# Keys turned in four full blocks, the last low block of v in full products, and the order planned anew

## The chip, the core and the metric

The program runs on one core of a Trainium2 chip. Its engines work side by side, each through its own queue in order: TensorE (PE, with its weight loads as PEld), VectorE (DVE), ScalarE (ACT), GpSimd (POOL), and SyncE (SP), which only issues transfers. The metric is device time of one execution in microseconds; less is better.

## The reference, cut to what matters

```python
def _attn_ref(q, k, v, g_q, g_k):            # 8 batches, 12 heads, 448 positions, head size 64
    q_n, k_n = rmsnorm(q, g_q), rmsnorm(k, g_k)
    scores = scale * np.matmul(q_n, k_n.transpose(0, 1, 3, 2))
    attn = np.exp(scores - np.max(scores, axis=-1, keepdims=True))
    attn = attn / (np.sum(attn, axis=-1, keepdims=True) + 1e-09)
    return np.matmul(attn, v)

def _moe_ref(x, w_in, conv_w, w_out):        # x: 8 x 448 x 768, w_in: 768 x 1024
    h = np.maximum(x @ w_in, 0.0)
    conv_out = ...                           # three taps along the sequence, one weight per column
    gate = 1.0 / (1.0 + np.exp(-conv_out))
    return h * gate @ w_out
```

The twelve heads of a batch are laid side by side to make its x.

## The kernel before

Two heads are worked on together; there are 48 such pairs, six to a batch. Most matrix products are done in float16 with operands that are split into a high and a low part, so that one product becomes three (high by high, low by high, high by low).

For pair n the steps are, by their names in the code:

- `load_k`, `load_q`, `square`, `square_sum`, `rsqrt` (nine small operations on 16 or 32 columns, numbered 0 to 8, each on DVE or POOL), `apply_rms`: the rows are normalised.
- `qk_transpose(n, 1)` turns the keys on TensorE, `qk_transpose(n, 0)` the queries, in four blocks each; 448 keys make three blocks of 128 rows and one of 64. `qk_hi` and `qk_lo` bring the result out of PSUM.
- `scores(n, g)` for g from 0 to 3: the products of queries and keys. Groups 0 to 2 use the two 64-row halves of the array at once, one head in each (the profile's form 64*128); group 3 uses the whole array.
- `soft_max` (DVE), `soft_exp` (ACT), and for pairs 10 to 47 `p_hi`, `p_lo` and `p_turn` (split the probabilities and turn them by a transfer). Pairs 0 to 9 are turned on TensorE by `p_transpose`, and `p_evac` brings them out.
- `pv(n, k)`: the product with v. Each matmul makes 64 columns of the result, one head in each 64-column half of the array, so they go in couples (form 128*64). For pairs 10 to 47 the table `PV7` lists eleven couples: block number, high or low part of v, and how many rows. Its entry for the low part of block 3 has 64 rows, the others 128.
- `sum_transpose` and its followers, `x_scale`, `x_hi`, `x_lo`: the sums and the pair's part of x.

For batch b, `in_part` is x by `w_in`, then `in_relu`, `in_conv`, `in_tanh`, `in_gate`, `in_hi`, `in_lo`, and `out_part` is the product with `w_out`.

All steps draw on eight PSUM banks. The order on every engine is not written out. A planner at the end of the function takes each step's due time (from the table `PH`), what it needs (`needs`), the engines it may run on and an estimate of its cost (`options`), and picks step by step. It adds 0.09 to a TensorE step whose `mode` differs from that of the step before. What it settles is fixed before the program runs: each engine then follows its list and waits where a list makes it wait. The engine that a step runs on comes from the same choice.

The last block of the keys' rows that is not filled by keys is set to zero once (`z[HALF[1], 1, :, :, 3]`), and `v_load` fills the matching rows of v's block 3 with the same 64 rows a second time.

Of the kernel before, what the change touches and what calls it, by code (L numbers as in the profile page):

```python
# [10 lines left out]
F32 = mybir.dt.float32  # L11
# [8 lines left out]
PH = dict(  # L20
    T0=10.967, N0=6, T=15.459, ti=17.476, si=5.11, so=8.471, hop=0.482, beta=0.03, wi0=-42.913,
    wi1=123.322, wo0=27.142, wo1=142.983, cw=-10.8, tg=-97.576, tl=35.262, ea=0.79, te=113.425,
    ep=0, hs=0, nf=3, adj=0.139, nz=8, ne=0, sc=5, tc=2, mc=8, p_qe=0.885, p_evac=1.078,
    p_hi=1.427, p_lo=9.771, p_rms=1.35, p_v=0.784, p_x=0.724, p_g=1.806, p_relu=0.483,
    p_cv=0.454, p_qz=0.683, p_ev=2.488, sp=0.083, nbulk=16, p_rs=0.002, p_sq=1.249, p_w=0.964,
    v0=-5.914, dg=7, n1=10, sw=-0.025, nl=4, tj=0.658, hk=0, pvs=1, pk=0.1, p_sa=0.456,
    p_ph=0.558, p_pl=0.0, nq=3, nk=94, p_qh=0.287, p_ql=0.313, tq=9.136, ti0=0.38, ti1=-0.226,
    ti2=-0.488, ti3=0.474, ti4=-0.143, ti5=0.702, ti6=0.881, ti7=-2.49, si0=1.104, si1=1.725,
    si2=1.798, si3=1.468, si4=1.613, si5=1.143, si6=1.624, si7=1.691, to0=0.944, to1=0.306,
    to2=-1.453, to3=-1.281, to4=-0.007, to5=-0.844, to6=-0.745, to7=-1.059, so0=1.501, so1=1.467,  # L30
    so2=1.988, so3=1.424, so4=1.513, so5=0.757, so6=0.754, so7=0.218, pg=0.05,
    dq=[-3.68, -0.12, 0.27, 2.41, 3.7, 2.72, 2.35, -4.24, 0.69, 8.02, -0.69, 3.34, -0.75,
# [3 lines left out]
    da=[-0.05, 0.22, 0.68, 2.21, 3.37, -3.05, -1.7, -0.58, -2.92, 0.62, 2.69, -0.09, 4.89,  # L36
# [3 lines left out]
    dv=[-1.03, -0.52, -1.1, -1.21, -4.04, -5.21, -6.35, 4.57, 7.65, 3.51, 2.52, -1.82,  # L40
# [3 lines left out]
)  # L44
# [22 lines left out]
def tile_attention_moe(ctx: ExitStack, tc, q, k, v, g_q, g_k, w_in, conv_w, w_out, out):  # L67
# [343 lines left out]
    def square_sum(n):  # L411
        m = duo(n)[0]
        w = D // 2 if halved(n) else D
        if m == n:
            new("st", n, [P, 4, duo(n)[1], 2, 2 * NB], F32)
        nc.vector.tensor_reduce(  # L416
            old("st", m)[:, 0, n - m].rearrange("p i s -> p (i s)"),
            old("sq", n).rearrange("p i h t d -> p (i h t) d")[..., :w], axis=AX.X, op=ALU.add,
        )
# [90 lines left out]
    def qk_transpose(n, i):  # L510
        ps = new_bank("t", ("qk", n, i))
        x = slots(n, i).rearrange("p t h d -> p t (h d)")
        for t in range(NB):
            m, w = (min(P, S - t * P), P) if i else (PB, PB)
            nc.tensor.transpose(ps[:, t * w : t * w + m], x[:m, t], ident[:m, :m])  # L515

# [148 lines left out]
    def nd(n):  # L665
        return 0 if n < PH["n1"] else PH["dg"]
# [125 lines left out]
    def sum_load(n, h):  # L792
# [10 lines left out]
    PV7 = (  # L803
        *((c, 0, P) for c in range(4)), *((c, 1, 64 if c == 3 else P) for c in range(4)),
        *((c, 0, P) for c in (4, 5, 6)),
# [333 lines left out]
    def needs(name, *a):  # L1139
# [300 lines left out]
    def options(name, *a):  # L1440
# [29 lines left out]
            apply_rms=lambda: [dve(0.68)] if a[0] < PH["ep"] else [pool(1.14), dve(0.68)],  # L1470
            qk_transpose=lambda: [pe(0.48)],
            apply_gain=lambda: [pool(1.14), dve(0.68)],
# [19 lines left out]
            sum_load=lambda: [dma("rb", 0.75)],  # L1492
            pv=lambda: [pe(2 * PV_STEP * 0.00082 * (S - nd(a[0]) * P // 2) if a[1] < NB else (0.77, 0.77, 0.58)[a[1] - NB])],
            x_scale=lambda: [dve(0.64)],
# [11 lines left out]
            in_carry=lambda: [dve(0.18), act(0.3)],  # L1506
            out_part=lambda: [pe(0.665)],
            out_evac=lambda: [act(0.58), dve(0.6)],
# [89 lines left out]
    free = dict.fromkeys(waiting, 0.0)  # L1598
    pmode = None

    def mode(name, *a):

        return name if name == "pv" or name == "scores" and a[1] != NG - 1 else ""

# [3 lines left out]
    def vacant(step, e, dma, t):  # L1608
# [64 lines left out]
    while len(order) < len(steps):  # L1673
        best = None
        for e, ws in waiting.items():
            pick = None
            for step, (t, _, dma) in ws.items():
                t = max(t, free[e])
                if dma and step[0] in BULK and len(bulk) >= PH["nbulk"]:
                    t = max(t, bulk[-PH["nbulk"]])  # L1680
                t, spots = vacant(step, e, dma, t)
                if t > 1e8:
                    continue
                sw = 0.0
                if e == "PE" and mode(*step) != pmode:
                    t += 0.09
                    sw = PH["sw"]
                elif locks(e, step[0], *step[1:2]):
                    t = max(t, port["DVE"] - PH["pk"] if e == "POOL" else port["POOL"] + PH["pg"])
                key = t + sw + (BETA if e != "SP" else PH["sp"]) * urgency(step), urgency(step), steps[step][1]  # L1690
                if pick is None or key < pick[0]:
                    pick = key, t, step, spots
            if pick and (best is None or pick[1] < best[0]):
                best = *pick[1:], e
# [88 lines left out]
```

## Time and profile before

| | |
|---|---|
| timed runs | 863.71, 863.99, 869.9 us; median 863.99 us |
| the profiled execution, from its first instruction to its last | 866.6 us |
| TensorE, matmuls in flight | 810.0 us, 5416 matmuls |
| DVE, ACT, POOL busy | 663.1, 680.0, 632.9 us |

The page gives each engine's busy time, the chain of work that ended last, and groups of instructions. Views of the trace give stretches of it: a row of a timeline has the start and the length of a run of instructions of one kind, so the difference between the starts of two rows that follow each other is what the first of them cost the engine. A matmul's own length in the trace is longer than that, since matmuls overlap in the array.

### The profile page before, as it was taken

The numbers are of one execution on the slowest core, as the hardware profiler recorded it, in microseconds if no ns is written. First come the engines' busy times: TensorE is split into PE (matmuls) and PEld (weight loads), VectorE is DVE, ScalarE is ACT, GpSimd is POOL, SyncE is SP. The second block draws the span as 40 slices with busy tenths as digits, with TensorE's granted clock in tenths as the row PEclk, the third lists the DMA queues.
The fourth block names the chain that finished last, engine by engine and source line by source line (L and its number), as shares of the span: only waits on it lengthen the run. The fifth ranks groups of instructions, "written<-read, shape, count | busy, mean of one in ns | idle before, by whom it ended". The sixth has DMA issues, their size and how long they took to land.

```text
span 866.6 us, 16129 instructions
## 1 busy us (share of the span) xinstructions
PE 810.0 (93%) x5416; PEld 416.0 (48%) x5416; DVE 663.1 (77%) x1100; ACT 680.0 (78%) x1476; POOL 632.9 (73%) x849
## 2 busy tenths in 40 slices
PE   0688899999999799999999999999999999999998
PEld 0244444544444355455445545545454555445554
DVE  5799889887888988888788887687888767772530
ACT  1689678987998888888899879889879788884541
POOL 6436647787889788887888788888889877974210
PEclk9999999999999899999999999999999999999999
DMA  8963844136989989996998899789998997566001
GB/s 233 268 203 73 204 120 81 36 79 128 196 181 186 189 159 194 172 185 142 214 185 143 171 203 200 149 171 171 195 194 142 175 171 143 115 106 131 37 1 73
DMA packets 338446, 132.63 MB, mean 153 GB/s; under 512 B 301908, under 2 KB 332988, under 8 KB 337596
## 3 DMA queue, kind: packets, MB, share of 16 engines
q1 hardware_dynamic: 338364, 131.60, 74.3%
q8 instruction: 43, 0.70, 0.3%
q14 instruction: 39, 0.32, 0.1%
HBM read 58.22 MB, written 11.18 MB: 80 GB/s over the span
## 4 chain that ended last, share of the span: by engine, by line
PE 82%; DVE 7%; ACT 3%; DMA 3%; SPq 3%; issue 2%; POOL 0%; DVEq 0%; ACTq 0%; POOLq 0%
PE banks L999 25%; PE banks L920 24%; PE banks L695 12%; PE banks L846 10%; PE banks L515 4%; PE banks L837 4%; PE banks L757 2%; DMA v<-in_v_dram 2%; ACT e L710 1%; SPq L380 1%; DVE vacc L616 1%; PE banks L777 1%; SPq L1096 1%; ACT PT L93 1%; DVE ph L105 1%
## 5 line engine op out<-in xcount | busy, mean ns | idle before, releaser
L105 POOL TENSOR_TENSOR ph<-e,ph 128x768 f16<-128x768 f32 (+3 forms) x296 | 270.5, 936 | 40.6 <-ACT ph L93 26.9
L920 PE MATMUL banks<-x,wi 128*128 128x448 f16 x1152 | 248.1, 353 | 0.3 <-ACT e L710 0.3
L999 PE MATMUL banks<-wo,gring 128*128 128x384 f16 (+1 forms) x1056 | 211.0, 329 | 4.7 <-ACT e L710 4.4
L920 PEld LDWEIGHTS <-wi 128*128 128x128 f16 x1152 | 108.8, 98 | 99.6 <-issue 12.9
L93 ACT CAST ph<-e 128x1024 f16<-128x1024 f32 (+1 forms) x147 | 137.7, 938 | 3.2 <-DMA PT<-ph 1.2
L999 PEld LDWEIGHTS <-gring 128*128 128x128 f16 (+1 forms) x1056 | 101.8, 100 | 73.8 <-issue 17.1
L695 PE MATMUL banks<-kT,qT 64*128 64x448 f16 x864 | 105.9, 358 | 5.5 <-DVE qT L553 4.2
L105 POOL TENSOR_TENSOR sq<-qk,st 128x512 f32<-128x512 f32 x96 | 103.2, 1090 | 5.8 <-DVE st L438 4.4
L846 PE MATMUL banks<-PT,vp 128*64 128x448 f16 (+1 forms) x836 | 97.6, 363 | 1.2 <-issue 0.9
L515 PE MATMUL banks<-ident,sq 128*128 128x128 f32 (+1 forms) x364 | 60.3, 278 | 20.9 <-POOL sq L105 18.4
L416 DVE TENSOR_REDUCE st<-sq 128x16 f32<-128x1024 f32 x48 | 58.1, 1210 | 13.8 <-ACT sq L399 13.7
L846 PEld LDWEIGHTS <-vp 128*64 128x64 f16 (+1 forms) x836 | 41.3, 109 | 52.8 <-issue 33.7
L515 PEld LDWEIGHTS banks<-ident,sq 128*128 128x128 f32 (+1 forms) x364 | 43.6, 144 | 45.5 <-POOL sq L105 21.8
L105 POOL TENSOR_TENSOR x<-rB,x 128x448 f16<-128x448 f32 x48 | 50.0, 1042 | 19.9 <-ACT x L93 19.3
L695 PEld LDWEIGHTS <-qT 64*128 64x128 f16 x864 | 34.4, 95 | 59.0 <-issue 31.8
L757 PE MATMUL banks<-ident,e 128*128 128x128 f32 x280 | 44.3, 291 | 9.8 <-ACT PT L93 2.9
L999 PE MATMUL banks<-wo,wi 128*128 128x384 f16 (+1 forms) x192 | 50.3, 327 | 0.0
L399 ACT ACTIVATE sq<-qk 128x1024 f32<-128x1024 f32 x41 | 43.1, 1052 | 7.9 <-DMA qk<-in_q_dram 5.0
L853 DVE TENSOR_TENSOR rB<-banks,rB 128x448 f32<-128x448 f32 x48 | 29.7, 619 | 25.2 <-PE banks L846 14.9
L93 ACT COPY PT<-banks 128x512 f32<-128x512 f32 x64 | 36.5, 582 | 13.1 <-PE banks L757 10.6
L757 PEld LDWEIGHTS banks<-ident,e 128*128 128x128 f32 x280 | 32.8, 146 | 27.9 <-ACT PT L93 8.3
L562 POOL COPY qz<-qT 64x128 f16<-64x128 f16 x96 | 30.3, 315 | 16.5 <-DVE qT L553 11.7
(1129 smaller groups left out, 1627.7 us busy)
## 6 DMA issues: line engine op xcount, KB each, us to landing
rB<-rd SPq DMA_DIRECT2D x96, 112.0 KB
qk<-in_q_dram SPq DMA_DIRECT2D x23, 448.0 KB
wo<-in_moe_w_in_dram SPq DMA_DIRECT2D x6, 1024.0 KB
v<-in_v_dram SPq DMA_DIRECT2D x24, 256.0 KB
gring<-in_moe_w_out_dram SPq DMA_DIRECT2D x8, 768.0 KB
qk<-in_k_dram SPq DMA_DIRECT2D x23, 256.0 KB
v<-in_v_dram SPq DMA_DIRECT2D x24, 192.0 KB
qk<-in_k_dram SPq DMA_DIRECT2D x23, 192.0 KB
```

What stands on the lines that cost most here:

```text
L93: (nc.scalar.copy if e == "ACT" else elementwise(e).tensor_copy)(dst, src)
L105: elementwise(e).tensor_tensor(dst, a, b, op=op)
L399: nc.scalar.activation(sq, qk(n), AF.Square)
L416: nc.vector.tensor_reduce(old("st", m)[:, 0, n - m].rearrange("p i s -> p (i s)"), old("sq", n).rearrange("p i h t d -> p (i h t) d")[..., ...
L515: nc.tensor.transpose(ps[:, t * w : t * w + m], x[:m, t], ident[:m, :m])
L562: e.tensor_copy(z[HALF[h], :, HALF[h]], old("qT", n)[HALF[h], :, t0 : t0 + 64])
L695: nc.tensor.matmul(ps[u][:, :S], lhs, kt[r, w], start=(i == 0), stop=(i == 2))
L757: nc.tensor.transpose(ps[:, kt * P : (kt + 1) * P], e[:, k0 : k0 + P], ident)
L837: nc.tensor.matmul(ps[HALF[h], :S], v[r, h, k], pt[r, k, h * S : (h + 1) * S], start=(k == 0), stop=(k == NB - 1),)
L846: nc.tensor.matmul(ps[HALF[h], :S], v[:m, w, h, c % 4], pt[:m, c, h * S : (h + 1) * S], start=(i == 0), stop=(i == len(PV7) - 1),)
L920: nc.tensor.matmul(ps[:, :S], wi[:, wl, c, fc * P : (fc + 1) * P], old("x", b * NP + c)[:, xl], start=(i == 0), stop=(i == 3 * NP - 1),)
L999: nc.tensor.matmul(ps[p0 : p0 + m, :NO2], g, wo[:, wl, fc, half * NO2 : (half + 1) * NO2], start=(i == 0), stop=(i == 3 * NFC - 1),)
```

## The change

`qk_transpose` turns the fourth block of the keys with all 128 rows, where it took 64. `PV7` takes 128 rows for the low part of block 3. The planner's charge for a change of tiling is made anew: a step now has a mode at its beginning and one at its end. `needs` and `ORDER` say that some steps, such as `square_sum` of two pairs, keep their order, and all numbers of `PH` and some costs in `options` are others, so that the lists of all engines are made anew.

```diff
 PH = dict(
-    T0=10.967, N0=6, T=15.459, ti=17.476, si=5.11, so=8.471, hop=0.482, beta=0.03, wi0=-42.913,
+    T0=11.0661, N0=6, T=15.4646, ti=17.4515, si=5.1142, so=8.4623, hop=0.4923, beta=0.0299,
...
     def square_sum(n):
         m = duo(n)[0]
         w = D // 2 if halved(n) else D
-        if m == n:
-            new("st", n, [P, 4, duo(n)[1], 2, 2 * NB], F32)
+        if ("st", m) not in rings.setdefault("st", Ring(BUFS["st"])).d:
+            new("st", m, [P, 4, duo(n)[1], 2, 2 * NB], F32)
...
         for t in range(NB):
-            m, w = (min(P, S - t * P), P) if i else (PB, PB)
-            nc.tensor.transpose(ps[:, t * w : t * w + m], x[:m, t], ident[:m, :m])
+            m = P if i else PB
+            nc.tensor.transpose(ps[:, t * m : (t + 1) * m], x[:m, t], ident[:m, :m])
...
     PV7 = (
-        *((c, 0, P) for c in range(4)), *((c, 1, 64 if c == 3 else P) for c in range(4)),
+        *((c, 0, P) for c in range(4)), *((c, 1, P) for c in range(4)),
         *((c, 0, P) for c in (4, 5, 6)),
     )
...
             yield "square_half", n
+            yield "square_sum", n - 1
...
         elif name == "qk_hi":
+            yield ("x_turn" if turned(n - 1, a[1]) else "qk_hi"), n - 1, a[1]
...
-            qk_transpose=lambda: [pe(0.48)],
+            qk_transpose=lambda: [pe(0.44 if a[1] else 0.39)],
...
-            out_part=lambda: [pe(0.665)],
+            out_part=lambda: [pe(0.652)],
...
-    pmode = None
-
-    def mode(name, *a):
-
-        return name if name == "pv" or name == "scores" and a[1] != NG - 1 else ""
+    pmode = "T"
+
+    def modes(name, *a):
+
+        if name == "scores" and a[1] != NG - 1:
+            return "SS"
+        if name == "pv":
+            return "VQ" if a[1] == NB - 1 else "VV"
+        if name == "out_part" and a[0] % 2 and not a[1]:
+            return "VV"
+        return "TT"
...
     ORDER = {
+        ("qk_hi", "qk_hi"), ("x_turn", "qk_hi"), ("square_sum", "square_sum"),
...
-                if e == "PE" and mode(*step) != pmode:
-                    t += 0.09
+                if e == "PE" and modes(*step)[0] != pmode:
+                    t += 0.094
```

Three places show what becomes of the lists. The names behind an arrow are what an instruction reads, those ahead of it what it writes; line numbers after the change are seven higher up to the middle of the file.

First TensorE in the middle of the program, where the keys of a pair are turned between products with `w_out` (`sq` holds the normalised rows, `gring` the gated hidden layer). Before:

```order
L777 MATMUL banks<-ident,rsum_4297 7x128
L515 MATMUL banks<-ident,sq_4081 128x128 x3
L515 MATMUL banks<-ident,sq_4081 128x64
L999 LDWEIGHTS gring
L999 MATMUL banks<-wo_82,gring 128x384
```

And after, at a like place:

```order
L1006 LDWEIGHTS gring
L1006 MATMUL banks<-wo_82,gring 128x384
L522 MATMUL banks<-ident,sq_4059 128x128 x4
L522 MATMUL banks<-ident,sq_4059 128x112 x4
L702 LDWEIGHTS qT_4259
```

The block of 64 columns is gone, and the keys are four alike; here the queries' four blocks of 112 follow at once.

Second DVE at the start of the program, from the sum of squares of pair 0 on (`st` holds the sums and what `rsqrt` makes of them, `wi` and `wo` the words of the first weight that `convert` works on). Before:

```order
L451 TENSOR_TENSOR st_133<-st_133 128x16
L453 TENSOR_TENSOR st_133<-st_133 128x16
L438 SCALAR_TENSOR_TENSOR st_133<-st_133 128x16
L243 TENSOR_SCALAR wi_81<-wo_82 128x1024
L247 SCALAR_TENSOR_TENSOR wi_81<-wo_82,wi_81 128x1024
L251 SCALAR_TENSOR_TENSOR wi_81<-wo_82,wi_81 128x1024
L243 TENSOR_SCALAR wi_81<-wo_82 128x1024
```

And after:

```order
L458 TENSOR_TENSOR st_133<-st_133 128x16
L460 TENSOR_TENSOR st_133<-st_133 128x16
L250 TENSOR_SCALAR wi_81<-wo_82 128x1024
L254 SCALAR_TENSOR_TENSOR wi_81<-wo_82,wi_81 128x1024
L258 SCALAR_TENSOR_TENSOR wi_81<-wo_82,wi_81 128x1024
L445 SCALAR_TENSOR_TENSOR st_133<-st_133 128x16
L250 TENSOR_SCALAR wi_81<-wo_82 128x1024
```

`rsqrt` 4 of pair 0 has gone from DVE to POOL, and `rsqrt` 8, the last, has come from POOL to DVE, behind the three instructions of the first block of the weight; POOL has 4 to 7 now where it had 5 to 8, six instructions in either case.

Third DVE in pair 40, from `soft_max` of group 1 to that of group 2 (`sst` is its result, `c_` the convolution, `o_` an output row, `ph` the split probabilities). Before:

```order
L701 TENSOR_REDUCE sst_(40_1_7663<-banks 128x1 x2
L958 SCALAR_TENSOR_TENSOR c_(5_5_7557<-c_(5_5_7557,banks 128x448
L948 SCALAR_TENSOR_TENSOR c_(5_6_7640<-banks,cwb_7054,c_(5_6_7640 128x447 x2
L416 TENSOR_REDUCE st_7702<-sq_7649 128x16
L99 TENSOR_SCALAR o_(4_2_7717<-banks,vsc_4327 128x384
L701 TENSOR_REDUCE sst_(40_2_7723<-banks 128x2
```

And after:

```order
L708 TENSOR_REDUCE sst_(40_1_7633<-banks 128x1 x2
L955 SCALAR_TENSOR_TENSOR c_(5_5_7618<-banks,cwb_7062,c_(5_5_7618 128x447 x2
L910 TENSOR_TENSOR vsc_5483<-vsc_5483,wsc 128x1
L918 COPY vsc_4407<-vsc_5483 64x1
L919 COPY vsc_4407<-vsc_4407 64x1
L569 COPY qz_78<-qT_7566 64x2x64
L945 TENSOR_SCALAR banks<-banks 128x448
L112 TENSOR_TENSOR ph_71<-e_74,ph_71 128x2x3x128
L112 TENSOR_TENSOR ph_71<-e_74,ph_71 128x2x64
L708 TENSOR_REDUCE sst_(40_2_7696<-banks 128x1 x2
```

Both instructions of a `p_lo` (the rows with `ph`) and a `q_middle` (`qz`) stand on DVE now, between two `soft_max`; before, they were on POOL.

## Rows read from the trace of the kernel before

**Rows 1.** The page: an engine's busy time, and the chain that ended last.

```profile
PE 810.0 (93%) x5416; PEld 416.0 (48%) x5416; DVE 663.1 (77%) x1100; ACT 680.0 (78%) x1476; POOL 632.9 (73%) x849
...
PE 82%; DVE 7%; ACT 3%; DMA 3%; SPq 3%; issue 2%; POOL 0%; DVEq 0%; ACTq 0%; POOLq 0%
```

**Rows 2.** Windows: length, busy PE, PEld, DVE, ACT, POOL, granted clock, DMA.

```profile
0.00:309.00 309.00, 256.69 (x1615) 129.80 (x1617) 264.35 (x440) 246.66 (x548) 219.16 (x297) 0.98 0.70 156
309.00:862.00 553.00, 552.71 (x3803) 286.11 (x3798) 398.71 (x662) 432.73 (x928) 413.71 (x553) 1.00 0.78 152
...
195.00:290.00 95.00, 92.97 (x611) 46.08 (x612) 79.55 (x133) 85.08 (x186) 81.19 (x108) 0.98 0.90 172
275.00:308.00 33.00, 26.88 (x176) 12.32 (x175) 29.51 (x54) 28.42 (x63) 28.41 (x34) 0.90 0.96 182
290.00:402.00 112.00, 106.41 (x743) 53.64 (x740) 95.67 (x162) 95.94 (x208) 95.29 (x128) 0.97 0.92 178
```

**Rows 3.** Timeline of TensorE at 439 us: start, length, line, tiles, form, count.

```profile
439.12 0.73 PE L920 MATMUL banks<-x,wi 128*128 128x448 f16 x3
439.79 0.74 PE L695 MATMUL banks<-kT,qT 64*128 64x448 f16 x6
440.46 0.74 PE L920 MATMUL banks<-x,wi 128*128 128x448 f16 x3
441.04 0.73 PE L695 MATMUL banks<-kT,qz 128*128 128x448 f16 x3
```

**Rows 4.** Timeline of TensorE: four blocks turned, and the row behind.

```profile
145.44 0.60 PE L757 MATMUL banks<-ident,e 128*128 128x128 f32 x4
145.88 1.87 PE L920 MATMUL banks<-x,wi 128*128 128x448 f16 x9
...
558.28 0.69 PE L515 MATMUL banks<-ident,sq 128*128 128x128 f32 x4
558.90 0.34 PE L999 MATMUL banks<-wo,wi 128*128 128x384 f16 x1
```

**Rows 5.** Timeline of TensorE: couples of `scores` and of `pv`.

```profile
414.42 1.31 PE L695 MATMUL banks<-kT,qT 64*128 64x448 f16 x12
415.66 2.12 PE L999 MATMUL banks<-wo,gring 128*128 128x384 f16 x12
...
492.79 0.76 PE L846 MATMUL banks<-PT,vp 128*64 128x448 f16 x6
493.38 0.33 PE L999 MATMUL banks<-wo,carry 128*64 128x384 f16 x1
...
536.79 2.51 PE L846 MATMUL banks<-PT,vp 128*64 128x448 f16 x22
539.23 0.74 PE L920 MATMUL banks<-x,wi 128*128 128x448 f16 x3
```

**Rows 6.** Timeline of TensorE: `out_part` of batch 1, first couple's second.

```profile
290.55 0.35 PE L999 MATMUL banks<-wo,gring 128*64 128x384 f16 x1
```

**Rows 7.** Timeline of all engines at the start.

```profile
10.73 0.68 POOL L451 TENSOR_TENSOR st<-st 128x16 f32<-128x16 f32 x1 [6.07 <-DVE st L438]
...
17.71 1.21 POOL L441 TENSOR_TENSOR st<-st 128x16 f32<-128x16 f32 x1
...
19.00 3.00 POOL L105 TENSOR_TENSOR sq<-qk,st 128x512 f32<-128x512 f32 x2
...
21.05 2.14 PE L515 MATMUL banks<-ident,sq 128*128 128x128 f32 x8 [17.41 <-POOL sq L105]
...
25.78 1.22 DVE L416 TENSOR_REDUCE st<-sq 128x16 f32<-128x1024 f32 x1 [5.68 <-ACT sq L399]
```

**Rows 8.** Groups of POOL by form: busy and mean ns, idle time before.

```profile
L440 POOL TENSOR_SCALAR st<-st 128x32 f32<-128x32 f32 x48 | 14.5, 303 | 9.8 <-DVE st L453 5.7 <-DVE st L438 0.4 <-DVE vsc L903 0.3
```

**Rows 9.** Groups of DVE by form: `p_lo` on DVE.

```profile
L105 DVE TENSOR_TENSOR ph<-e,ph 128x128 f16<-128x128 f32 x4 | 5.7, 1415 | 0.0
...
L105 DVE TENSOR_TENSOR ph<-e,ph 128x768 f16<-128x768 f32 x4 | 4.4, 1088 | 0.4 <-issue 0.4
```

More of the change, by code (lines that the diff above doesn't have):

```diff
@@ L20 @@
 PH = dict(
-    T0=10.967, N0=6, T=15.459, ti=17.476, si=5.11, so=8.471, hop=0.482, beta=0.03, wi0=-42.913,
[L22 to L32, printed above, removed]
[3 rows of a table removed]
@@ L36 @@
-    da=[-0.05, 0.22, 0.68, 2.21, 3.37, -3.05, -1.7, -0.58, -2.92, 0.62, 2.69, -0.09, 4.89,
[3 rows of a table removed]
-    dv=[-1.03, -0.52, -1.1, -1.21, -4.04, -5.21, -6.35, 4.57, 7.65, 3.51, 2.52, -1.82,
[3 rows of a table removed]
+    T0=11.0661, N0=6, T=15.4646, ti=17.4515, si=5.1142, so=8.4623, hop=0.4923, beta=0.0299,
+    wi0=-41.2827, wi1=119.1785, wo0=27.9545, wo1=143.8054, cw=-9.6684, tg=-90.8517,
+    tl=32.789, ea=0.7918, te=217.3462, ep=0, hs=0, nf=3, adj=0.2276, nz=8, ne=0, sc=5, tc=2,
+    mc=8, p_qe=4.1115, p_evac=1.1526, p_hi=1.3939, p_lo=7.3877, p_rms=0.28, p_v=0.7109,
@@ new lines @@
+    p_x=0.7745, p_g=1.7978, p_relu=0.6212, p_cv=0.0433, p_qz=0.0, p_ev=1.9625, sp=0.0742,
+    nbulk=19, p_rs=0.0, p_sq=1.313, p_w=0.7634, v0=-6.0597, dg=7, n1=10, sw=-0.023, nl=4,
+    tj=0.8241, hk=0, pvs=1, pk=0.1, p_sa=0.6508, p_ph=1.3427, p_pl=0.0, nq=3, nk=94,
+    p_qh=1.9342, p_ql=0.0, tq=5.84, ti0=-0.3161, ti1=0.037, ti2=-0.322, ti3=2.1597,
+    ti4=-3.4032, ti5=0.6195, ti6=1.7483, ti7=0.4464, si0=1.1151, si1=1.7223, si2=1.7949,
+    si3=1.4674, si4=1.5955, si5=1.0881, si6=1.5356, si7=3.7477, to0=-0.6062, to1=0.3318,
@@ L44 @@
+    to2=-2.2678, to3=-0.9684, to4=1.7365, to5=0.0885, to6=-5.8445, to7=1.2481, so0=1.6134,
+    so1=1.4693, so2=2.0138, so3=1.4856, so4=1.5042, so5=0.6157, so6=0.6172, so7=0.4225,
+    pg=0.0,
+    dq=[0.4741, 0.2577, 0.3372, 1.6476, 3.9318, 19.8106, 2.7901, -5.5699, 2.814, 7.3983,
[5 rows of a table added]
+    da=[-0.1608, -1.2419, 1.791, 42.3961, 17.0007, -3.371, -1.1798, -0.2757, -1.5319,
[5 rows of a table added]
+    dv=[-2.2334, 0.6027, -0.9272, 1.3287, -2.4816, -4.752, -5.1356, 4.9615, 8.039, 4.3052,
[4 rows of a table added]
 )
@@ L1492, in options @@
             sum_load=lambda: [dma("rb", 0.75)],
-            pv=lambda: [pe(2 * PV_STEP * 0.00082 * (S - nd(a[0]) * P // 2) if a[1] < NB else (0.77, 0.77, 0.58)[a[1] - NB])],
+            pv=lambda: [pe((0.75, 0.75, 0.75, 0.85)[a[1]] if a[1] < NB else (0.76, 0.76, 0.57)[a[1] - NB])],
             x_scale=lambda: [dve(0.64)],
@@ L1498, in options @@
             out_scales=lambda: [dve(0.35)],
-            in_part=lambda: [pe(0.58)],
+            in_part=lambda: [pe(0.568)],
             in_relu=lambda: [act(0.53), dve(0.62)],
@@ L1701, in tile_attention_moe @@
         if e == "PE":
-            pmode = mode(*step)
+            pmode = modes(*step)[1]
         tag, got = taken[step]
```

23 rows, old and new, of tables (da, dq, dv) are left out of this document.

## The prediction

> **What bounds the kernel now.** I read the page first, then windows by stage, then timelines of TensorE. The page puts PE at 810.0 us of a span of 866.6 and gives it 82% of the chain that ended last [rows 1]. That alone would not say that a shorter PE list ends sooner, so the windows matter more: from 309 us to 862 us PE has 552.71 us of 553.00 filled at a granted clock of 1.00, while DVE, ACT and POOL are busy for 399, 433 and 414 us [rows 2]. There PE waits for nobody, and each 0.1 us taken out of its list comes off the end. The first 309 us are of another kind: PE is busy for 256.7, DVE for 264.4 [rows 2], and PE's waits are holes that other engines leave. A saving on PE may vanish into such a hole. The span goes on for some 4 us behind that, with the last outputs, which nothing here touches.
>
> **What a change of tiling costs.** At 439.12 us three matmuls over the whole array are followed by `scores` in 64-row halves, and the next row starts 0.67 us later; at 440.46 the same three are followed by group 3, which uses the whole array, and the next row starts 0.58 us later [rows 3]. So the change costs 0.09 to 0.10 us. The way back costs as much: six `scores` matmuls in three couples take 0.67 us to the next start [rows 3], and twelve take 1.24 [rows 5], so three couples more are 0.57, a couple is 0.19, and the first six hold 0.10 more than three couples. The Trainium skill says of it, in TensorEngine Tiling (Array Packing), section Key Properties, that changing the tiling mode drains the engine, and gives no price; the trace agrees, at about 0.1 us.
>
> Written out matmul by matmul, the PE list of before has 526 changes of tiling. That order with the two wider blocks would have 374, and the new order has 367. So nearly all of the effect on tiling is the padding, and the planner's new charge brings seven changes.
>
> **Keys in four full blocks.** Four blocks of the keys, the last of 64 rows, take 0.62 us from their start to the next row; four full blocks of `p_transpose`, the same operation on the same type, take 0.44 [rows 4]. The saving is 0.18 each. The 64 columns more that the block streams are already in the 0.44. It holds where a whole-array step comes next, as in 36 of the 48 pairs. In six the next step is a couple in column halves, and only one of two changes goes (0.09 saved); in six it is `scores`, whose tiling the small block shared, and a change is added (0.1 lost). 36 x 0.18 + 6 x 0.09 - 6 x 0.10 = **6.4 us**. Bringing the result out is as before, since only 448 columns are read.
>
> **Low block of v in full products.** The 22 matmuls of `pv` take 2.44 us to the next start [rows 5]. Three couples of `pv` without a change inside take 0.59 [rows 5]; eight couples more at 0.19 and one change on leaving at 0.10 make 0.59 + 1.52 + 0.10 = 2.21. The difference, 0.23, is the change into the 64-row form and out of it. 38 pairs x 0.23 = **8.7 us**. The operands have 128 rows already, so nothing is loaded or split more. Seven changes fewer by the order: 7 x 0.1 = **0.7 us**. In all PE's list is 15.8 us shorter.
>
> Pairs 0 to 18 have their keys turned, and pairs 10 to 15 their `pv`, before the first output product of batch 1, at 290.55 us [rows 6]: 19/48 of 6.4 and 6 x 0.23 make 3.9 us in the stage where PE has holes. Its worth is between 0 and 3.9; I take 2, since from 195 to 290 us PE is busy for 93.0 of 95.0 [rows 2], near to the full stage, and before that it isn't. The other **11.9 us** lie under a full PE.
>
> **The start.** PE's first transposes start at 21.05 us, after a wait of 17.4 for POOL's `apply_rms` [rows 7]. POOL runs six `rsqrt` instructions before it from 10.73 to 18.92, then two `apply_rms` until 22.0 [rows 7]. They are long because DVE works on the weight at the same time: the small ones take 0.68 to 1.7 us here, and on twice as many columns later in the program 0.30 on average [rows 8]. In the new order DVE does the first block of the weight, three instructions until about 13.5, and then has to wait for POOL, because `rsqrt` 8 stands next on its list. Queued behind that wait are the second and third blocks of the weight and `square_sum` of pair 1. While DVE waits, POOL works alone: two instructions until about 13.4, four more at 0.3, so 14.7, DVE's step 0.2, two `apply_rms` in 3.0 with the first ready after half of it. PE starts near 17 instead of 21. DVE loses about 1.5 us to the wait, but in the old order it stands still for 5.68 us before `square_sum` of pair 1, waiting for ACT's square [rows 7], which on ACT's list stands behind the first keys. So the lost time lies in a gap that exists, and the gap itself comes earlier. The gain is between 0 (if the loads, which begin as before, or DVE's queue set the next steps) and 4; I take **3**.
>
> **Work moved to DVE.** 15 more `p_lo` are on DVE (19, from 4), 13 `apply_rms`, 13 `q_middle`, 7 `in_relu`, 5 `qk_hi`, 4 `out_evac`, 3 `in_lo`. One `p_lo` on DVE took 1.09 + 1.42 = 2.5 us [rows 9], so 15 x 2.5 = 37; the rest, at 0.2 to 0.7 each, is about 22. DVE goes from 663 to some 723 us of 850, and POOL gets freer by as much. By stretches, the list adds 11 us to DVE's 79.6 of 95 from 195 to 290 us (95%) and 5 to 95.7 of 112 from 290 to 402 (92% of a stretch that is 3 us shorter) [rows 2]. DVE stays below PE, but from 195 to 400 us hardly. What would pay is `soft_max` behind a `p_lo` in DVE's queue, then `soft_exp`, then the bank that PE wants. I take **3 us** of new waits there; the bounds are 0, as in the 553 us where DVE at 72% stops nobody, and 9, the price of a hole like that of 275 to 308 us: PE busy for 26.9 of 33.0, 6.1 idle, at a granted clock of 0.90 [rows 2], so some 3 more.
>
> On the rest of PE's list the distances are much as they were: from the turned queries to their `scores` at least 2.0 us of PE work after pair 13 (0.7 before), from group 3 of `scores` to `pv` at least 10.7 (9.5 before), from `in_part` to the product that reads it at least 5.3 (5.3).
>
> **Sum.** -11.9 - 2 - 3 + 3 = -13.9 us. The profiled execution spans 866.6 us, so 852.7; the median of the timed runs, 863.99, lies 2.6 below it. 863.99 - 13.9 = **850 us**. With every term at its good end it is 863.99 - 11.9 - 3.9 - 4 = 844, at its bad end 863.99 - 11.9 + 9 = 861.
>
> **Rivals.**
> 1. *The holes come back twice.* DVE at 92 to 95% makes two holes like that of 275 to 308 us, each 9 us, in place of the 3 that I allowed: 850 - 3 + 18 = 865. For it: the load of DVE, and that in the old order this stretch broke already. Against it: DVE had less left there in places without any hole. Chance 0.12.
> 2. *Slower: `p_lo` in front of `soft_max`.* The place is DVE's list as in pair 40, at any of the 15 new ones. If each holds `soft_max` back by its 2.5 us and 2.0 of it reaches PE, that is 30 us: 850 - 3 + 30 = 877. It decides when DVE has less than 2.5 us left between two groups of `scores`; with 8 to 12% of a pair's 15 us left, it has 1.2 to 1.8 in a pair, so it needs all of the lateness to reach PE with no bank in reserve. Against it: in the old trace three of the four such `p_lo` lie in the full stretch, where PE never stood. Chance 0.06.
> 3. *Better: the early stage closes up.* The hole of 275 to 308 us goes too, 9 us, and no new wait comes: 850 - 3 - 9 = 838. For it: the new order has other steps there (`pv` of pair 15 stands ahead of all `scores` of pair 17, where it stood between their first two groups). Chance 0.10.
> 4. *The padding costs instead of saving.* The Trainium skill, in TensorE: Matmul & The Clock Gate, section Back-to-back issue gap, has the gap between matmuls grow with the number of moving columns, so a block with 64 more would take longer. As a mechanism of this kernel: if what makes the four key blocks slow isn't the tiling, a wider block adds half of the 0.11 us of a full one, 48 x 0.055 = 2.6 us, and the 6.4 are not won: 850 + 9 = 859. The rows speak against it, since four full blocks take less than three full ones and a small one [rows 4]. Chance 0.03.
>
> **How the numbers follow.** The forecast, 850 with its own range of 844 to 857, has 0.69. A measurement of this kernel can tell about 1% from no change, so faster means below 855.4. The forecast gives 0.65 to that and 0.04 to the same, rival 3 gives 0.10 and rival 1 a hundredth or two if only one of its holes comes; rival 4 and most of rival 1 are within 1%; rival 2 is slower, as is rival 1 with a third hole (0.02). Faster 0.77, same 0.15, slower 0.08. The range of 839 to 862 leaves out rival 2, most of rival 1 and the far part of rival 3, 0.2 together.
>
> **What would show it.** In the changed kernel's profile, the four key blocks should take 0.44 us to the next start and the 22 matmuls of `pv` 2.2; PE should be full from about 300 us to the end, and that stretch should be some 12 us shorter; the first transposes should start near 17 us. If the keys and `pv` take what they did, the price of tiling is wrong. If they are shorter and the time isn't, rows of PE with waits for ACT's `soft_exp` or DVE will show where it went, and DVE's `p_lo` should stand before them. I would also be wrong if the earlier start is eaten before 290 us, which the first output product of batch 1 would tell: it should come some 4 us sooner.

## The result, and the profile after

The changed kernel takes 855.86 us (median of four runs, 854.89 to 857.72), against 865.4 us for the kernel before (863.71 to 869.9). The ratio is 0.9876, with a 95% interval of 0.9833 to 0.9919. So the kernel became faster by some 9.5 us by the medians, and by 10.7 if one goes by the ratio. The forecast was 13.9 us less, 850 us; the time lies inside the range given, but 0.5 us above 855.4, and the prediction had put it below that with a chance of 0.77. Two thirds to three quarters of the forecast gain came, and the question is where the other 3.2 to 4.4 us went.

The page of the changed kernel (busy time of each engine, then the chain that ended last), which answers to [rows 1]:

```profile
PE 798.1 (93%) x5416; PEld 422.4 (49%) x5416; DVE 715.5 (84%) x1194; ACT 671.6 (78%) x1460; POOL 594.6 (69%) x779
...
PE 77%; DVE 12%; ACT 4%; issue 2%; DMA 2%; POOL 2%; SPq 0%; POOLq 0%; DVEq 0%; ACTq 0%
```

PE has 11.9 us less to do and DVE 52 us more. PE's share of the chain fell from 82% to 77%, DVE's rose from 7% to 12%: more often than before, the end now hangs on DVE.

The windows of the changed kernel, which answer to [rows 2] (length, busy time of PE, PEld, DVE, ACT and POOL, granted clock, DMA share, GB/s):

```profile
0.00:309.00 309.00, 259.75 (x1635) 133.46 (x1637) 276.15 (x458) 250.90 (x558) 216.38 (x296) 0.96 0.71 158
275.00:308.00 33.00, 25.23 (x173) 12.14 (x171) 30.32 (x49) 28.96 (x65) 25.75 (x37) 0.84 0.91 176
...
309.00:845.00 536.00, 531.58 (x3745) 285.11 (x3740) 439.32 (x737) 418.99 (x900) 378.23 (x484) 1.00 0.80 155
```

Two things differ from [rows 2]. The hole of 275 to 308 us is still there and a little deeper: PE busy for 25.23 of 33 instead of 26.88, at a granted clock of 0.84 instead of 0.90. And the stretch behind it is no longer full: 4.42 us of 536 are empty, where before 0.29 of 553 were.

The timeline of the changed kernel's TensorE: four key blocks and four blocks of the queries with the row behind each, then the 22 matmuls of `pv` and the first output product of batch 1. They answer to [rows 4 to 6].

```profile
434.68 0.60 PE L522 MATMUL banks<-ident,sq 128*128 128x128 f32 x4
435.12 0.73 PE L927 MATMUL banks<-x,wi 128*128 128x448 f16 x3
...
458.45 0.55 PE L522 MATMUL banks<-ident,sq 112*128 112x112 f32 x4
458.83 0.73 PE L927 MATMUL banks<-x,wi 128*128 128x448 f16 x3
...
282.69 2.27 PE L853 MATMUL banks<-PT,vp 128*64 128x448 f16 x22
284.89 1.31 PE L702 MATMUL banks<-kT,qT 64*128 64x448 f16 x12
286.13 0.74 PE L927 MATMUL banks<-x,wi 128*128 128x448 f16 x3
286.80 0.35 PE L1006 MATMUL banks<-wo,carry 128*64 128x384 f16 x1
```

A row's worth is read from start to start. The keys take 435.12 - 434.68 = 0.44 us (0.62 before), `pv` 284.89 - 282.69 = 2.20 (2.44 before). Both are what was forecast, 0.44 and 2.21. The first output product of batch 1 starts at 286.80 us instead of 290.55.

Where the time went is best seen at two marks: the start of `scores` of pair 18, at the end of the early stage, and that of the first output product of batch 7, 36 us ahead of the end. Each number is a row's start in the timeline of TensorE of that kernel's profiled run; the kernels below the second are the experiments of the next section.

| kernel | `scores`, pair 18 | batch 7's first output product | between |
|---|---|---|---|
| before | 306.64 | 830.62 | 523.98 |
| changed | 303.70 | 820.03 | 516.33 |
| paddings alone, old order (e1) | 299.50 | 812.19 | 512.69 |
| the same with the new start (e7) | 302.38 | 815.13 | 512.75 |
| keys' padding alone, old order (e3) | 304.84 | 828.47 | 523.63 |
| `pv`'s padding alone, old order (e4) | 304.66 | 822.46 | 517.80 |
| new order alone (e2) | 307.07 | 832.92 | 525.85 |
| changed, a second time (e9) | 305.98 | 822.34 | 516.36 |
| changed, all shared work to POOL (e5) | 304.93 | 820.60 | 515.67 |
| changed, late shared work to POOL (e10) | 304.55 | 818.73 | 514.18 |
| changed, from pair 18 on (e12) | 303.32 | 817.35 | 514.03 |

Read the columns with care. The changed kernel's two profiles, the second row and e9's, lie 2.3 us apart at the first mark and 0.03 us apart between the marks. So one profile can't tell 2 us in the early stage, and it can tell a few tenths in the long one.

From before to changed, the early stage is 2.9 us shorter (0.7 by e9) and the long one 7.7, where 11.9 was expected of the latter. So 4.2 us are missing behind pair 18, in the stretch that the prediction took for safe. The timeline shows two waits there. The first, with all engines (the number in brackets is the idle time before and what ended it):

```profile
420.06 2.76 POOL L112 TENSOR_TENSOR sq<-qk,st 128x512 f32<-128x512 f32 x2 [1.14 <-DVE st L445]
...
420.14 4.81 DVE L112 TENSOR_TENSOR ph<-e,ph 128x768 f16<-128x768 f32 x2 [0.17 <-ACT ph L100]
...
422.78 2.02 POOL L112 TENSOR_TENSOR ph<-e,ph 128x768 f16<-128x768 f32 x2
...
424.88 0.61 DVE L708 TENSOR_REDUCE sst_(25_3_4755<-banks 128x1 f32<-128x448 f32 x1
...
425.52 0.63 ACT L717 ACTIVATE e<-banks,sst_(25_3_4755 128x448 f32<-128x448 f32 x1 [3.08 <-DVE sst_(25_3_4755 L708]
...
426.39 0.57 PE L522 MATMUL banks<-ident,sq 112*128 112x112 f32 x4 [1.64 <-ACT e L717]
```

Read it from the end: PE waits 1.64 us for a bank that `soft_exp` on ACT gives back; ACT waited 3.08 for `soft_max` on DVE; and DVE stood in a `p_lo` for 4.81 us. That `p_lo` ends at 424.95, as POOL's run of `apply_rms` and its own `p_lo` ends at 424.80. The second wait is of the same make:

```profile
743.58 2.03 POOL L112 TENSOR_TENSOR ph<-e,ph 128x768 f16<-128x768 f32 x2
...
743.68 3.33 DVE L569 COPY qz<-qT 64x128 f16<-64x128 f16 x1
...
745.54 0.28 POOL L569 COPY qz<-qT 64x128 f16<-64x128 f16 x1
...
745.80 1.17 POOL L112 TENSOR_TENSOR ph<-e,ph 128x384 f16<-128x384 f32 x2
746.94 0.67 DVE L955 SCALAR_TENSOR_TENSOR c_(6_3_8829<-banks,cwb,c_(6_3_8829 128x447 f32<-128x447 f32 x1
...
747.64 0.19 DVE L569 COPY qz<-qT 64x128 f16<-64x128 f16 x1
...
749.75 0.73 PE L927 MATMUL banks<-x,wi 128*128 128x448 f16 x3 [1.82 <-DVE c_(6_3_8829 L965]
```

One `q_middle` copy on DVE takes 3.33 us, and the next one, of the same shape, 0.19. The long one ends within 0.1 us of POOL's last row beside it. Behind it the convolution is late, and PE waits 1.82 us. Both waits are in e9 too, with 1.64 and 1.80 us. The two waits are 3.46 us of the 4.42 that are empty.

### The profile page after: what moved, and what is told of

It reads as the page before. It is cut to its first block, busy times and chain, and to the rows that moved or that the text cites. A ratio compares the mean times of both kernels' runs of the same rounds, so it can differ in the third digit from the quotient of the medians.

```text
span 855.7 us, 16123 instructions
## 1 busy us (share of the span) xinstructions
PE 798.1 (93%) x5416; PEld 422.4 (49%) x5416; DVE 715.5 (84%) x1194; ACT 671.6 (78%) x1460; POOL 594.6 (69%) x779
## 4 chain that ended last, share of the span: by engine, by line
PE 77%; DVE 12%; ACT 4%; issue 2%; DMA 2%; POOL 2%; SPq 0%; POOLq 0%; DVEq 0%; ACTq 0%
PE banks L1006 24%; PE banks L927 23%; PE banks L702 12%; PE banks L853 8%; PE banks L522 4%; PE banks L844 3%; PE banks L764 2%; ACT e L717 1%; DVE qz L569 1%; DVE ph L112 1%; DMA wo<-in_moe_w_in_dram 1%; DVE wi L254 1%; DVE wi L258 1%; DMA rB<-rd 1%; POOL ph L112 1%
## 5 line engine op out<-in xcount | busy, mean ns | idle before, releaser
L112 POOL TENSOR_TENSOR ph<-e,ph 128x128 f16<-128x128 f32 (+3 forms) x266 | 245.5, 945 | 55.5 <-ACT ph L100 30.4
L1006 PE MATMUL banks<-wo,gring 128*128 128x384 f16 (+1 forms) x1056 | 206.2, 327 | 0.0
L100 ACT CAST ph<-e 128x1024 f16<-128x1024 f32 (+1 forms) x151 | 141.4, 937 | 2.2 <-DMA PT<-ph 0.4
L1006 PEld LDWEIGHTS <-gring 128*128 128x128 f16 (+1 forms) x1056 | 102.2, 99 | 68.7 <-issue 11.3
L702 PE MATMUL banks<-kT,qT 64*128 64x448 f16 x864 | 108.2, 362 | 6.3 <-DVE qT L560 4.3
L112 POOL TENSOR_TENSOR sq<-qk,st 128x512 f32<-128x512 f32 (+1 forms) x83 | 93.2, 1138 | 7.2 <-DVE st L445 6.0
L853 PE MATMUL banks<-PT,vp 128*64 128x448 f16 x836 | 88.8, 359 | 0.8 <-DMA PT<-ph 0.8
L522 PE MATMUL banks<-ident,sq 128*128 128x128 f32 (+1 forms) x364 | 54.7, 279 | 22.4 <-POOL sq L112 14.7
L853 PEld LDWEIGHTS <-vp 128*64 128x64 f16 x836 | 44.7, 111 | 39.1 <-issue 11.6
L100 ACT COPY PT<-banks 128x512 f32<-128x512 f32 x64 | 36.7, 584 | 13.3 <-PE banks L764 13.0
L406 ACT ACTIVATE sq<-qk 128x1024 f32<-128x1024 f32 x37 | 39.0, 1054 | 7.7 <-DMA qk<-in_q_dram 5.1
L860 DVE TENSOR_TENSOR rB<-banks,rB 128x448 f32<-128x448 f32 x48 | 29.6, 616 | 13.7 <-PE banks L853 9.4
L112 DVE TENSOR_TENSOR ph<-e,ph 128x768 f16<-128x768 f32 (+3 forms) x38 | 34.4, 946 | 4.8 <-ACT ph L100 4.4
```

Source lines behind the costliest of these rows:

```text
L100: (nc.scalar.copy if e == "ACT" else elementwise(e).tensor_copy)(dst, src)
L112: elementwise(e).tensor_tensor(dst, a, b, op=op)
L406: nc.scalar.activation(sq, qk(n), AF.Square)
L522: nc.tensor.transpose(ps[:, t * m : (t + 1) * m], x[:m, t], ident[:m, :m])
L702: nc.tensor.matmul(ps[u][:, :S], lhs, kt[r, w], start=(i == 0), stop=(i == 2))
L853: nc.tensor.matmul(ps[HALF[h], :S], v[:m, w, h, c % 4], pt[:m, c, h * S : (h + 1) * S], start=(i == 0), stop=(i == len(PV7) - 1),)
```

## Experiments

The theory: the gain is the padding's, at the size forecast, and the new order takes some of it back. Its rival: the padding brings less than forecast, and the order is neutral or helps. Each change can be had alone, since the order is a list that the kernel builds before it issues anything. Labels stand ahead of each experiment; intervals are at 95%, and each ratio is to the kernel before on the same chip.

**e1: both paddings in the old kernel, order untouched.**

```diff
-            m, w = (min(P, S - t * P), P) if i else (PB, PB)
-            nc.tensor.transpose(ps[:, t * w : t * w + m], x[:m, t], ident[:m, :m])
+            m = P if i else PB
+            nc.tensor.transpose(ps[:, t * m : (t + 1) * m], x[:m, t], ident[:m, :m])
...
-        *((c, 0, P) for c in range(4)), *((c, 1, 64 if c == 3 else P) for c in range(4)),
+        *((c, 0, P) for c in range(4)), *((c, 1, P) for c in range(4)),
```

> The order of before with both paddings and nothing else. Theory A (a change of tiling costs PE about 0.1 us, and the waits that ate part of the gain belong to the new order): PE's list is 15 us shorter, and all but 1 to 2 of it reaches the end, so about 13 us less than before, ratio 0.984 to 0.986, faster than the changed kernel. Theory B (whatever shortens PE's list meets engines that are nearly full, so the waits come in any order): about 10 us less, ratio 0.988. Theory C (the gain is the new order's): 4 us less at most, ratio 0.995 or more. In the trace the 22 matmuls of pv should take 2.2 us to the next start and the four key blocks 0.44, by A and B.

**e2: the changed kernel with both paddings taken back** (the same lines, the other way).

> The changed kernel without the two paddings, its order kept. Theory A: PE's list is 15 us longer than in the changed kernel, and nearly all of it shows where PE is full: 867 to 870, ratio to before 1.000 to 1.005. Theory B: with the old list's length the waits go, so about as before, ratio 0.997 to 1.000. Theory C: near the changed kernel, ratio 0.990.

**e3 and e4: the old kernel with one padding each**, the keys' and `pv`'s.

> The order of before with the keys' fourth block full, and pv as before. Theory A: 6.4 us off PE's list, of which 4 lie under a full PE and part of the other 2.4 counts: 4 to 6 us less, ratio 0.993 to 0.995. The rival in which the padding costs: 2 to 3 us more, ratio 1.003.

> The order of before with the low part of v's last block in 128 rows, and the keys as before. Theory A: 38 x 0.23 = 8.7 us off PE's list, nearly all under a full PE: 7.5 to 8.7 us less, ratio 0.990 to 0.992. If the price of tiling is smaller in pv than read: 4 us less or none.

| | ratio to before | interval | us off 866.1 |
|---|---|---|---|
| e1, both paddings, old order | 0.9842 | 0.9823 to 0.9861 | -13.7 |
| e2, new order, no padding | 1.0038 | 1.0024 to 1.0053 | +3.3 |
| e3, keys alone | 0.9935 | 0.9916 to 0.9955 | -5.6 |
| e4, `pv` alone | 0.9911 | 0.9895 to 0.9927 | -7.7 |

The last column is (ratio - 1) x 866.1 us, the median of the kernel before in these runs. The two paddings add up within their intervals: 5.6 + 7.7 = 13.3, and 13.7 together; the keys' part is the loosest, since e3's twelve runs spread from 856.95 to 866.48 us. The order by itself costs 3.3. The theory holds in the main, and its rival is out: the old order with the paddings is faster than the changed kernel. In measured time e1's interval overlaps the changed kernel's first one and lies below its second, 0.9874 to 0.992 (e9 below). The table of marks says it more sharply for the long stretch: e1 has 512.69 us there, 11.3 less than before, and the padding's share of the forecast was 11.9 - 0.7 = 11.2. (The profiled run of e1 is its fastest, 850.15 us against a median of 853.21, so its early mark says some 3 us too little.)

What the order costs depends on the length of PE's list, though. Behind pair 18 it is 525.85 - 523.98 = 1.9 us without the paddings and 516.33 - 512.69 = 3.6 with them. In e2 the first late wait is there with 1.20 us, and the second is not: PE is full from 745 to 770 us. So about half of the late loss appears only with order and paddings together, and not with the order alone.

Nor is such a hold-up a matter of the new order alone. The profiled run of e3, the slowest of its twelve, has the order and the engines of before:

```profile
617.64 5.30 DVE L823 SCALAR_TENSOR_TENSOR vp<-v,vsc,vp 128x512 f16<-128x512 f32 x1
618.01 2.04 POOL L105 TENSOR_TENSOR ph<-e,ph 128x768 f16<-128x768 f32 x2
...
624.04 0.64 ACT L710 ACTIVATE e<-banks,sst_(38_0_7228 128x448 f32<-128x448 f32 x1 [3.81 <-DVE sst_(38_0_7228 L701]
...
626.38 0.27 PE L777 MATMUL banks<-ident,rsum 128*7 128x128 f32 x1 [3.19 <-DVE rsum L774]
```

An instruction on v (`vp`), on DVE in every version, took 5.30 us, where it mostly takes 0.74, beside POOL rows without a gap; `soft_max` came behind it, and PE waited 3.19 us. That is most of what is missing between e3's marks, 0.3 us less than before where 29/48 of 6.4, 3.9 us, could be expected.

**What in the order costs?** The two late waits suggest that instructions of `p_lo`, `apply_rms` and `q_middle` that the new plan put on DVE are held up by POOL's, and that what stands behind them comes late (theory D in the expectations). Against it stands that this work costs nothing as long as it is done early enough, and that the loss comes from the order of the steps. e5 gives all of them to POOL and keeps the order of the steps.

```diff
+    for step in order:
+        if step[0] in ("p_lo", "apply_rms", "q_middle"):
+            on[step] = "POOL"
     SCHED.update(
```

> The changed kernel with every p_lo, apply_rms and q_middle on POOL, as before the change; the order of all steps is kept, and the lists of PE, ACT and SP stay word for word. Theory D (the new order's waits come from such instructions on DVE, each held up while POOL works, with soft_max or another step that PE needs behind it): the waits of PE near 424, 748 and 297 us go, and most of the 7 us between the changed kernel and the old order with paddings comes back: ratio to before 0.980 to 0.984. Theory E (POOL's load or the order itself makes the waits): as the changed kernel or slower, ratio 0.987 to 0.992, with PE waiting for POOL or the transfers behind it.

**e5a: `p_lo` alone to POOL** (the same loop, with `step[0] == "p_lo"`).

> The changed kernel with every p_lo on POOL and nothing else moved. If p_lo, the longest of the moved instructions, makes the waits: nearly all of what the run with all three kinds moved gives, with the wait near 424 us gone and the one near 748 us (behind a q_middle that took 3.3 us) still there. If the short ones matter as much: about half of it, ratio 0.984 to 0.987. Theory E: 0.987 or more.

e5 gave 0.987 (0.9842 to 0.9898), e5a 0.9888 (0.9868 to 0.9908): neither is told apart from the changed kernel, so in this wide form the theory fell. In e5 both late waits are gone, but the first output product of batch 1 starts at 290.74 us instead of 286.80. Its windows:

```profile
0.00:309.00 309.00, 256.90 (x1616) 131.40 (x1617) 262.62 (x438) 249.01 (x552) 227.44 (x310) 0.96 0.71 156
309.00:845.00 536.00, 533.93 (x3758) 285.99 (x3757) 407.99 (x693) 421.43 (x906) 414.40 (x534) 1.00 0.81 156
```

Behind 309 us PE's empty time fell from 4.42 to 2.07 us, but the time between the marks by only 0.7 us, as four other waits of 0.3 to 0.6 us stand in this stretch. Ahead of 309 us PE got through less, 256.90 instead of 259.75. That POOL delivers the early work later would fit this, but it isn't shown: e9, with the work on DVE, has 257.86 there, its first output product of batch 1 at 288.67 and its mark of pair 18 at 305.98, which is later than e5's 304.93. In e5a the wait near 750 us stays with 1.79 us, since `q_middle` is still on DVE there.

**e6 and e7: the start.** e6 is the changed kernel with `rsqrt` 4 and 8 of pair 0 back on their old engines; e7 is e1 with the two changed over as in the new order.

```diff
+    on["rsqrt", 0, 4], on["rsqrt", 0, 8] = "DVE", "POOL"
...
+    on["rsqrt", 0, 4], on["rsqrt", 0, 8] = "POOL", "DVE"
```

The first line is e6's, the second e7's.

> The changed kernel with rsqrt 4 of pair 0 back on DVE and rsqrt 8 back on POOL, as in the start of before. If the earlier start is worth what I took it for: PE's first transposes start 3 to 4 us later, near 20 us, and the whole is 3 us longer, ratio 0.991. If the start is eaten by 90 us, as the trace of the changed kernel looks: the first transposes come later, and the time is as in the changed kernel, ratio 0.986 to 0.989.

> The old order with both paddings, and with the new start: rsqrt 4 of pair 0 on POOL, rsqrt 8 on DVE behind the first block of the weight. If an earlier start is kept to the end in an order with fewer waits: 2 to 4 us less than the old order with paddings, ratio 0.980 to 0.982. If it is eaten in the first 100 us whatever the order: the same as that, 0.984.

e6 gave 0.9905 (0.9882 to 0.9927), e7 0.9806 (0.9784 to 0.9828). e7 has the best ratio of all. e6 lies 0.0008 above the changed kernel's own second measurement (below) and 0.0029 above the first, e7 lies 0.0036 below e1, which ran on another chip; the intervals overlap each time. A worth of the start between 0 and 3 us fits all four, and more can't be said.

**e9 to e11: the changed kernel again, and two more.** e10 moves the shared work to POOL only where POOL has room, from pair 20 on (e5's loop with `and step[1] >= 20`). e11 is e1 with the start pushed further: all of `rsqrt` from 4 to 8 and both `apply_rms` of pair 0 on DVE, right behind `rsqrt` 3, ahead of the weight.

```diff
+    first = [("rsqrt", 0, i) for i in range(4, NRS)] + [("apply_rms", 0, i) for i in (1, 0)]
+    for step in first:
+        on[step] = "DVE"
+        order.remove(step)
+    i = order.index(("rsqrt", 0, 3)) + 1
+    order[i:i] = first
```

> The changed kernel once more, beside the two others of this call, to have its ratio on one chip with theirs: 0.986 to 0.989, whatever the theory.

> The changed kernel with p_lo, apply_rms and q_middle on POOL from pair 20 on, and as in the changed kernel up to pair 19. Theory D in its narrower form (in the late stage, where POOL has room, these instructions on DVE cost PE its waits; in the early stage POOL has no room for them, which is why moving all of them gained nothing): the waits near 424 and 748 us go, the first output product of batch 1 stays near 287 us, and the whole is 3 to 4 us shorter than the changed kernel, ratio 0.982 to 0.985. If the moves only change where the waits are: as the changed kernel.

> The old order with both paddings, and rsqrt 4 to 8 and both apply_rms of pair 0 on DVE, ahead of the first block of the weight. If the start is kept to the end, as the run with only rsqrt 8 moved suggests: the first transposes start near 13 us, 7 to 8 us before the old start, and the whole is 5 to 6 us shorter than the old order with paddings, ratio 0.976 to 0.979. If DVE, which loses 3 us of its own list, sets the next steps: 0.980 to 0.982, as with the new start.

The changed kernel gave 0.9897 (0.9874 to 0.992) this time, e10 0.9882 (0.9854 to 0.991), e11 0.9838 (0.9814 to 0.9863). e10's windows around the two places of the late waits, and the long stretch:

```profile
410.00:430.00 20.00, 20.00 (x143) 10.26 (x139) 15.59 (x28) 17.63 (x41) 17.27 (x23) 1.00 1.03 203
735.00:755.00 20.00, 19.86 (x128) 10.52 (x126) 17.89 (x28) 15.14 (x34) 16.76 (x21) 1.00 0.56 96
...
309.00:845.00 536.00, 534.12 (x3759) 286.58 (x3760) 411.03 (x693) 419.93 (x903) 411.07 (x529) 1.00 0.80 155
```

The same two windows of the changed kernel:

```profile
410.00:430.00 20.00, 18.36 (x125) 9.41 (x123) 17.04 (x28) 15.13 (x35) 11.95 (x16) 1.00 0.84 173
735.00:755.00 20.00, 18.18 (x119) 9.76 (x118) 19.68 (x28) 13.73 (x30) 15.79 (x17) 1.00 0.47 93
```

Both holes, 1.64 and 1.82 us, are closed, and between the two marks e10 needs 514.18 us instead of 516.33 and 516.36. So for the late waits the theory is shown, though in the measured time its 1.3 us (0.0015 x 865.8) lie inside the intervals. e11 shows what a start that is earlier still is worth. Its timeline of TensorE:

```profile
11.77 1.83 PE L515 MATMUL banks<-ident,sq 128*128 128x128 f32 x8 [8.15 <-DVE sq L105]
17.53 0.56 PE L695 MATMUL banks<-kT,qT 64*128 64x448 f16 x2 [3.93 <-ACT qT L93]
23.98 0.93 PE L695 MATMUL banks<-kT,qT 64*128 64x448 f16 x4 [5.90 <-DVE qT L553]
...
37.76 1.30 PE L695 MATMUL banks<-kT,qT 64*128 64x448 f16 x6
```

The transposes come 4.1 us sooner than in e7 (15.88 there), but PE then waits 3.93 us for ACT and 5.90 for DVE; by the last row it is 0.4 us ahead of e7's 38.17. So ACT and DVE set the next steps, not the transposes, and in time e11 is not told apart from e1.

**e12: the same as e10 from pair 18 on**, to take in the hole near 290 us as well.

> As the run with the shared instructions on POOL from pair 20 on, but from pair 18 on, so that apply_rms of pair 18, which took 1.9 us on DVE in the hole near 297 us with PE waiting 1.6 for it, and three q_middle of pairs 18 and 19 go to POOL too. If they make the hole of the new order between 285 and 305 us longer than the old order's: PE's wait for DVE there goes, and the whole is 1.5 to 2.5 us shorter than with pair 20, ratio 0.984 to 0.987. If the hole is the order's (PE waits for soft_exp whoever does these steps): the same as with pair 20, 0.988, with the wait of 3 us for soft_exp still there.

e12 gave 0.9857 (0.9829 to 0.9884), not told apart from e10 either. Its window over the hole, and its long stretch:

```profile
280.00:310.00 30.00, 23.39 (x173) 11.71 (x173) 28.68 (x48) 27.22 (x61) 26.54 (x38) 0.89 0.94 180
...
309.00:845.00 536.00, 534.86 (x3763) 286.49 (x3760) 405.55 (x689) 419.65 (x901) 412.10 (x532) 1.00 0.82 156
```

The changed kernel over the same 30 us, and TensorE's and DVE's rows in it:

```profile
280.00:310.00 30.00, 22.88 (x171) 11.46 (x171) 27.28 (x46) 25.72 (x56) 23.99 (x35) 0.83 0.93 181
```

```profile
293.03 0.38 PE L784 MATMUL banks<-ident,rsum 128*7 128x128 f32 x1 [3.26 <-ACT e L717]
...
295.06 0.48 PE L1006 MATMUL banks<-wo,carry 128*64 128x384 f16 x1 [1.65 <-DVE c_(1_6_3072 L965]
...
296.06 1.90 DVE L112 TENSOR_TENSOR sq<-qk,st 128x512 f32<-128x512 f32 x1
...
298.11 1.27 PE L522 MATMUL banks<-ident,sq 128*128 128x128 f32 x5 [1.55 <-DVE sq L112]
```

In the changed kernel the hole is three waits in a row. The third, 1.55 us for an `apply_rms` that takes 1.90 on DVE, goes in e12, and the granted clock over the window is 0.89 instead of 0.83; the first two, 3.26 and 1.75 in e12, stay. So one part of the hole is the shared work, and the larger part, 3.26 us for `soft_exp`, is not.

## Why the prediction was right, and where it was not

- **A change of tiling costs 0.09 to 0.10 us.** Right. The prices worked out from it, 0.18 us for a pair's keys and 0.23 for its `pv`, stand in the rows of the changed kernel, and as times in e3 and e4: 5.6 us (3.9 to 7.3) where 6.4 was written, 7.7 where 8.7 was. Those two were the sums off PE's list, and the prediction counted 13.9 of 15.8 as reaching the end; e1 has 13.7 without the seven changes that the order saves.
- **The 11.9 us under a full PE.** Right for the old order: e1 and e7 are 11.3 and 11.2 us shorter between the marks, against 11.2 for the padding's part. In the changed kernel only 7.7 came.
- **Work moved to DVE, 3 us.** This is the step that failed, in place above all. The prediction put 3 us of new waits between 195 and 400 us and took 0 for what follows, "as in the 553 us where DVE at 72% stops nobody". With the new order DVE is busy there for 439.32 of 536 us, 82%, and 3.5 us of waits came in just that stretch, 4.2 us by the marks; that this is near the 3 written for another place is chance. How busy DVE is doesn't explain them by itself: a `p_lo` took 4.81 us and a copy of 0.19 took 3.33, both until POOL's work beside them was through. The prediction priced a `p_lo` on DVE at 2.5 us from its rows [rows 9], and a full one took less on average, 2.0; it was the longest that cost. A `q_middle` was priced with the rest at 0.2 to 0.7; the mean of the 13 on DVE was 0.94. The sign was in [rows 9]: the small part of a `p_lo`, 128 columns, took 1.42 us there and the part of 768 only 1.09, and of the 4.81 us the small part took 3.11.
- **The start, 3 us.** The first transposes start at 16.39 us instead of 21.05, near the 17 forecast, but in this run not by the way forecast. Two rows, the first of the changed kernel's first profile, the second of e9:

```profile
14.96 3.35 POOL L112 TENSOR_TENSOR sq<-qk,st 128x512 f32<-128x512 f32 x2 [2.66 <-DVE st L445]
...
14.48 0.18 DVE L445 SCALAR_TENSOR_TENSOR st<-st 128x16 f32<-128x16 f32 x1 [1.05 <-POOL st L448]
```

In the first, the weight's first block starts on DVE only at 11.53 us, POOL is through with its six `rsqrt` at 12.3, and it is POOL that waits for DVE. In e9, where that block starts at 10.23, DVE waits for POOL as forecast, and PE starts at 16.22. The old start is not fixed either: with it the transposes start at 17.81 us in e1 and 18.04 in e4. What the new one is worth came out as not told from 0. In the changed kernel `scores` of pair 0 start at 20.00 us instead of 23.8, but `scores` of pair 4 at 90.81 instead of 90.78. Against e6, the same order with the old start, pair 0 is 2.0 us earlier, pair 4 1.7, and pair 9 no longer (168.88 and 168.51). This is the doubt named at the end of the prediction. The tell-tale named with it, batch 1's first output product some 4 us sooner, did appear (3.75 us) and was misleading, since e1 has it at 283.7 us without the new start and e9 at 288.67 with it.
- **The order as a whole.** By the prediction -0.7 - 3 + 3 = -0.7 us. e2 measured +3.3 (2.1 to 4.6), and the changed kernel stands 0.0034 and 0.0055 above e1 in its two measurements, 2.9 and 4.8 us. From -0.7 to +3.3 is 4.0 us, which covers what is missing.
- **Rivals.** Rival 2, `p_lo` in front of `soft_max`, happened, but at one place of the 15, and reached PE with 1.64 us where 2.0 was written. Rival 1 did not come as two holes; the one that existed grew by 1.65 us of idle PE. Rival 3 did not come, since the hole stayed. Rival 4 is out by e3 and by the rows: a wider block saves. The Trainium skill's rule on changes of tiling, in TensorEngine Tiling (Array Packing), section Key Properties, decided here, and its rule on moving columns, in TensorE: Matmul & The Clock Gate, section Back-to-back issue gap, did not: 64 more columns came with 0.18 us less.

Three things stay open. From 30 to 130 us the granted clock was 0.91 in the changed kernel and in e9 and e10, where it was 1.00 before and in e1, 0.93 to 0.97 in the other kernels with the old order and 0.88 to 0.93 in the others with the new one; whether the early waits make this or follow from it was not separated, nor was what it costs. And e10 and e12 still need 1.3 to 1.5 us more between the marks than e1. And whether the hold-up seen in e3's slowest run is what spreads its twelve times was not separated.

Of the versions tried, the old order with both paddings is the best: 0.9842 in e1, 0.9806 with the new start in e7.

## What to carry to other kernels

Where TensorE is full, look for small blocks that force another tiling among full ones, and try them at full width: 0.1 us for each change that goes comes off the end, nearly one for one. When such an edit comes with an order made anew, measure the two apart, since the order can quietly take back a quarter of the gain. An engine at 80% isn't free for more work if that work is of the kind another engine holds up: look at the longest instruction of a group, not at its mean, and at what ran beside it. And where the early stage of one kernel moves by 2 us from run to run, read nothing of that size there from one profile.

## What the runs showed of the hardware

A DVE instruction can be held up for far longer than one instruction of POOL. The copy of 64x128 that takes 0.19 us took 3.33, through five POOL instructions in a row (two of `p_lo`, a copy, two more of `p_lo`), and ended with the last of them; the instruction on v in e3 took 5.30 where it mostly takes 0.74. The Trainium skill, in SBUF — State Buffer, section Who interferes with whom, says that the two engines share a pair of ports, and that against a DVE instruction in a mode that uses both pairs, as a copy may, whoever issues first has the shared pair for its whole instruction, while the other fully blocks. Which mode this copy ran in, no run here shows. The trace agrees on the blocking; by the rule the copy could have gone on after the first POOL instruction (1.66 us is the mean of the 98 of its form), and it did not.

The granted clock over a hole moved with the waits in it: 0.83 from 280 to 310 us with three waits, 0.89 with two (e12). The output products behind the second wait took 0.48 to 0.53 us where they take 0.33 in the full stretch.
